# Keys and values through TensorE tiles of 64x32, eight key and value loads in flight, and vp evacuated in two halves: memory attention and SwiGLU on one core

## The chip, the cores and the metric

One core of a Trainium2 chip runs the whole kernel as one program. The metric is the device time of one execution in microseconds. The kernel before took 909.95 us, the median of three runs (909.52, 909.95 and 912.1). Below, "engine" is one of TensorE (PE), VectorE (DVE), ScalarE (ACT), GpSimd (POOL) and the queue of SyncE (SP), which here issues the DMAs.

## The reference, cut to what matters

```
# q, k, v: (8 batches, 8 heads, 576 rows, 64), phi: (8, 8, 576, 32)
a = exp(phi - max(phi, rows));  a = a / (sum(a, rows) + 1e-9)
k_m = einsum('bhsm,bhsd->bhmd', a, k)        # 32 x 64 for each batch and head
v_m = einsum('bhsm,bhsd->bhmd', a, v)
s = q @ k_m.T / sqrt(64);  s = exp(s - max(s));  attn = s / (sum(s) + 1e-9)
x = (attn @ v_m), heads side by side         # 4608 tokens x 512
xn = x / sqrt(mean(x*x) + 1e-6) * rms_g
out = (silu(xn @ w_gate) * (xn @ w_val)) @ w_out     # 512 -> 1536 -> 512
```

All inputs are float32; the weights come in as float64 words that the kernel takes apart itself.

## The kernel before, in words

The kernel never builds x. It keeps the attention weights of each token (32 for each of 8 heads, so 256 for two head groups) and multiplies the weights by v_m first: vp = v_m @ (w_gate | w_val). The gate and value of a token are then its attention weights times vp. Float32 products in this second part are made from a high and a low half (the names end in h and l), in three matmuls each.

**Stage 1** (the pool ps1, lines 434 to 786) works through the 8 batches, and batches 2i and 2i+1 form pair i. For each batch `prep` loads phi, takes its maximum over the rows (`mc`, `mt`, `mx`, `mr`: a reduction, a transpose, a reduction, a transpose back), subtracts it and writes exp to `e_bd`. There each head pair (of 4) has 9 chunks of 64 columns: rows 0 to 63 of the partitions are the first head, with its exponentials in columns 0 to 31 and zeros beside them, and rows 64 to 127 are the second head, with zeros first. `kv_steps` multiplies: each matmul takes such a 128x64 block as its stationary operand and 64 columns each of k and v of both heads as the moving one, so 36 matmuls a batch (line 573) accumulate into `kvp`. `sums` (588) adds up the exponentials with a column of ones, over partial sums `es` that POOL has made (554, 556). `post1` (596 to 605) divides and masks: `im` is the reciprocal by a mask of heads, `kb` and `vb` are k_m and v_m by it. `turn` transposes them, `post2` copies them to `km` and `vt`, `self_products` and `post3` make the gram matrix of v_m that the norm needs, and `vg`, v_m scaled by rms_g, goes into `vm` in high and low halves (pairs 0 and 1) or to DRAM (`vgd`, pairs 2 and 3).

For the pairs 0 and 1 stage 1 also makes the scores: `q_steps` transposes q, `score_steps` multiplies by `km` into the PSUM tile `S`, and takes max, exp and sum. `x_steps` then transposes the attention weights (`tp`, `at`), makes the sums of squares with the gram matrix (`xp`, `ssq`), takes the reciprocal root by Newton steps on DVE (`rinv`, `u`), spreads it with `rp`, and splits the result into `ath` and `atl`. Beside this, `convert` turns a loaded weight block (`raw`) from float64 words into a float32 pair: five or six DVE operations, the source lines 345 to 385 in each (`ex`, `mi`, `w`), two ACT operations between, a cast on ACT (402) and a subtraction on POOL (403).

**Stage 2** (the pool ps2) loops over i from 0 to 47: two halves of the feed-forward width for each of 12 blocks by two pairs, twice. `vw_steps(i)` makes `vp` (840: 12 matmuls into one PSUM tile of 2x2x256 floats a partition, with one buffer) and `evac` splits it, per half of the partitions, into `xh` (an ACT cast, 853) and `xl` (a DVE subtraction, 854). `gv_steps` multiplies by `ath` and `atl` into `pg` and `pv` (876), takes silu and the product, and splits `hf` into `hh` and `hl`. `out_steps` multiplies by the output weights into `po` (918) and adds into `acc` (925). The pairs 2 and 3 have their scores made here, between the steps.

**What sets the order.** Each step has a due time in the table `PRM` (K_AT: a batch's products; KD: how far ahead of them each key and value tile is loaded; S_AT: scores; X_AT: the x steps; CV: conversions). Steps are recorded in that order, and a scheduler then places the instructions of each engine in one fixed row, which the chip runs in order. The input loads of stage 1 (`load`) stand in a chain of their own on SP: none is issued ahead of the one recorded before it. A load of `kv` (two DMAs, k and v of a head pair) also waits until the matmuls that read the buffer's former tile are through; there are 5 such buffers. On the same queue stand the stores of `vgd`, of the gram matrix (`gd`) and of converted weights (`wd`, `od`), and a store that waits for its data holds up every load behind it.

Of the kernel before, what the change touches and what calls it, by code (L numbers as in the profile page):

```python
# [31 lines left out]
    KD=[-29.43, -117.84, -35.71, -6.98, -5.97, -14.4, 0.19, -2.47, -27.9, -16.32, -19.75, -7.2, -11.66, -11.87, -26.49, -25.1, -22.49, -18.77, -23.35, -24.43, -11.42, -13.48, -5.56, -9.46, -16.01, -22.32, -10.3, -18.0, -66.41, -9.39, -2.35, -17.36],  # L32
    QD=[5.05, 6, 3, 5, 23.44, 20.6, 19, 15.8],
# [18 lines left out]
    B=[2, 2, 2],  # L52
# [38 lines left out]
def kernel(  # L91
# [25 lines left out]
    nc = tc.nc  # L117
# [28 lines left out]
    km_late = {b: persist.tile([P, HP, 64], F32, name=f"km{b}") for b in range(2 * G, B)}  # L146
    ssqs = {}
# [280 lines left out]
    with ExitStack() as c1:  # L428
# [8 lines left out]
        hmask = sb.tile([P, 2], F32, name="hmask", bufs=1)  # L437
        for g in range(4):
            for c in range(2):
                nc.vector.memset(hmask[32 * g:32 * g + 32, c:c + 1], float(g % 2 == c))  # L440
# [50 lines left out]
        def prep(b, hp0=0, hp1=HP):  # L491
# [46 lines left out]
            def s3():  # L538
                ph = st["phi", b][:, hp0:hp1]
                e = e_bd[b % 2]  # L540
                for h in range(2):
                    nc.scalar.activation(
                        e[64 * h:64 * h + 64, hp0:hp1, :, 32 * h:32 * h + 32],
                        ph[64 * h:64 * h + 64], AF.Exp,
                    )

            def s4():
                e = e_bd[b % 2]
                n = PRM["ESN"][b]
                es = []  # L550
                if n:
                    t = sk.tile([P, HP, 2, 64], F32, tag="es", name=f"es{b}")
# [9 lines left out]
        def kv_steps(b):  # L562
            j = b % 2

            def chunk(cc, c0, c1):
                def f():
                    if (cc, c0) == (0, 0):
                        st["kvp", b] = ps.tile([P, 2, 256], F32, tag="kx", name=f"kvp{b}", bufs=PRM["B"][1])
                    kvp = st["kvp", b]
                    for c in range(c0, c1):  # L570
                        for par in range(2):
                            hp = 2 * cc + (par ^ j)
                            nc.tensor.matmul(  # L573
                                kvp[64 * par:64 * par + 64, cc, 0:128],
                                e_bd[j][:, hp, c, :],
                                st["kv", b, hp][:, :, 64 * c:64 * c + 64],
                                start=(c == 0), stop=(c == NT - 1),
                            )
                return f

            def sums():
                kvp = st["kvp", b]
                for cc in range(2):
                    for par in range(2):
                        hp = 2 * cc + (par ^ j)
                        es = st["es", b]
                        for i, x in enumerate(es):
                            nc.tensor.matmul(
                                kvp[64 * par:64 * par + 64, cc, 128:129],
                                x[:, hp, :], ones, start=(i == 0), stop=(i == len(es) - 1),  # L590
                            )

            def post1():
# [4 lines left out]
                im = sb.tile([P, 2, 2], F32, tag="im", name=f"im{b}")  # L598
                nc.vector.tensor_tensor(
                    out=im, in0=si.broadcast_to([P, 2, 2]),  # L600
                    in1=hmask.unsqueeze(1).broadcast_to([P, 2, 2]), op=ALU.mult,
                )
                st["kb", b] = [sb.tile([P, 2, 2, 64], F32, tag=f"{x}b", name=f"{x}b{b}") for x in "kv"]
                for i in range(2):
                    nc.vector.tensor_tensor(
                        out=st["kb", b][i],
                        in0=kvp[:, :, 64 * i:64 * i + 64].unsqueeze(2).broadcast_to([P, 2, 2, 64]),
                        in1=im.unsqueeze(3).broadcast_to([P, 2, 2, 64]),
                        op=ALU.mult,
                    )  # L610

            def turn():
                kb = st["kb", b]
                st["kvt", b] = tp = ps.tile([P, 2, HP, 64], F32, tag="kx", name=f"kvt{b}", bufs=PRM["B"][1])
                for i in range(2):
                    for cc in range(2):
                        nc.tensor.transpose(
                            out=tp[:, i, 2 * cc:2 * cc + 2, :].rearrange("p s m -> p (s m)"),
                            in_=kb[i][:, cc].rearrange("p h d -> p (h d)"), identity=ident,
                        )  # L620

            def post2():
                tp = st.pop(("kvt", b))
                km = km_late.get(b)
                if km is None:
                    km = sb.tile([P, HP, 64], F32, tag="km", name=f"km{b}", bufs=4)
                nc.scalar.copy(km, tp[:, 0])
# [478 lines left out]
```

## Time and profile before

| what | us |
|---|---|
| median of three runs | 909.95 |
| the profiled execution | 910.09 |
| its span, first to last instruction | 908.3 |
| PE busy | 838.9 |
| DVE busy | 592.2 |
| ACT busy | 421.1 |
| POOL busy | 286.6 |

The span of the profiled execution is 1.8 us shorter than the execution, which lies 0.14 us from the median. The mean granted clock of TensorE is 0.969. The share of busy time says little by itself here, since two stages with different limits follow one another: stage 2 begins with the first `pg` matmul at 156.9 us. A row of the windows view gives, for a stretch of time, the busy us of each engine with the number of its instructions in brackets, the granted clock, the busy share of the DMA engines and GB/s. In the view by shapes a row gives line, engine, operation, output and inputs, count, then busy us and the mean ns of one, then the idle time just before them and what ended it. The chain of waits is the work that ended last, followed back from the end; "issue" in it is time in which the engine waited for nothing that the profile shows. A float32 matmul that isn't a transpose appears in the trace as two pieces, so the 36 products of a batch are 72 MATMULs.

### The profile page before, as it was taken

The numbers are of one execution on the slowest core, as the hardware profiler recorded it, in microseconds if no ns is written. First come the engines' busy times: TensorE is split into PE (matmuls) and PEld (weight loads), VectorE is DVE, ScalarE is ACT, GpSimd is POOL, SyncE is SP. The second block draws the span as 40 slices with busy tenths as digits, with TensorE's granted clock in tenths as the row PEclk, the third lists the DMA queues.
The fourth block names the chain that finished last, engine by engine and source line by source line (L and its number), as shares of the span: only waits on it lengthen the run. The fifth ranks groups of instructions, "written<-read, shape, count | busy, mean of one in ns | idle before, by whom it ended". The sixth has DMA issues, their size and how long they took to land.

```text
span 908.3 us, 15828 instructions
## 1 busy us (share of the span) xinstructions
PE 838.9 (92%) x6207; PEld 744.3 (82%) x6207; DVE 592.2 (65%) x1026; ACT 421.1 (46%) x717; POOL 286.6 (32%) x242
## 2 busy tenths in 40 slices
PE   4989485899989999899999999999999999999997
PEld 3777474889887899788888997798889999999996
DVE  5577968997898877988754655632445455454543
ACT  2656433777766464665543343254424333243330
POOL 3463745333333324234242241412112121121120
PEclk9889887999999999999999999999999999999999
DMA  8976543553464341634214134411204012040046
GB/s 284 324 254 236 201 157 96 182 185 86 153 166 132 106 119 61 165 110 153 89 58 140 35 94 128 97 55 47 93 1 140 1 48 93 1 140 1 1 111 144
DMA packets 81506, 106.41 MB, mean 117 GB/s; under 512 B 34324, under 2 KB 52248, under 8 KB 81432
## 3 DMA queue, kind: packets, MB, share of 16 engines
q1 hardware_dynamic: 81432, 105.41, 37.6%
q8 instruction: 49, 0.80, 0.4%
q14 instruction: 25, 0.20, 0.1%
HBM read 73.93 MB, written 31.46 MB: 116 GB/s over the span
## 4 chain that ended last, share of the span: by engine, by line
PE 74%; DVE 14%; issue 4%; DMA 4%; ACT 3%; POOL 1%; SPq 0%; DVEq 0%; ACTq 0%; POOLq 0%
PE po L918 29%; PE pv L876 14%; PE pg L876 14%; PE vp L840 7%; PE kvp L573 3%; PE xp L235 1%; DVE mi L365 1%; DVE xl L854 1%; DVE ex L345 1%; DVE w L385 1%; ACT xh L853 1%; PE qtp L685 1%; DVE mi L369 1%; DVE acc L925 1%; DMA phi<-in_phi_dram 1%
## 5 line engine op out<-in xcount | busy, mean ns | idle before, releaser
L899 POOL TENSOR_TENSOR hl<-hf,hh 128x512 fp32r<-128x512 f32 (+1 forms) x96 | 139.6, 1454 | 410.9 <-ACT hh L898 399.6
L925 DVE TENSOR_TENSOR acc<-po,acc 128x512 f32<-128x512 f32 x180 | 123.1, 687 | 130.2 <-PE po L918 129.5
L918 PE MATMUL po<-oh,hh 128*128 128x512 f32 x432 | 173.6, 403 | 3.6 <-DVE acc L925 2.6
L918 PE MATMUL po<-oh,hl 128*128 128x512 f32 x432 | 171.1, 396 | 0.0
L918 PE MATMUL po<-ol,hh 128*128 128x512 f32 x432 | 170.9, 396 | 0.0
L884 ACT ACTIVATE sg<-pg 128x256 f32<-128x256 f32 x192 | 77.7, 409 | 163.2 <-PE pg L876 144.2
L854 DVE TENSOR_TENSOR xl<-vp,xh 64x1024 fp32r<-64x1024 f32 x96 | 117.2, 1220 | 45.9 <-ACT xh L853 44.4
L885 DVE TENSOR_TENSOR hf<-pv,sg 128x256 f32<-128x256 f32 x192 | 85.3, 453 | 73.0 <-PE pv L876 51.1
L853 ACT CAST xh<-vp 64x1024 fp32r<-64x1024 f32 x96 | 96.6, 1007 | 51.7 <-PE vp L840 21.6
L898 ACT CAST hh<-hf 128x512 fp32r<-128x512 f32 (+1 forms) x96 | 64.6, 673 | 82.3 <-DVE hf L885 57.0
L918 PEld LDWEIGHTS po<-oh,hl 128*128 128x128 f32 x432 | 81.5, 189 | 19.5
L918 PEld LDWEIGHTS po<-oh,hh 128*128 128x128 f32 x432 | 81.5, 189 | 19.3 <-DVE acc L925 4.5
L876 PE MATMUL pg<-ath,xh 128*128 128x320 f32 (+1 forms) x384 | 86.6, 299 | 7.9 <-ACT xh L853 6.3
L918 PEld LDWEIGHTS po<-ol,hh 128*128 128x128 f32 x432 | 81.7, 189 | 11.5 <-DMA ol<-od 0.2
L840 PE MATMUL vp<-wh,vm 128*128 128x256 f32 x384 | 85.5, 288 | 4.8 <-DVE at L212 2.3
L876 PE MATMUL pv<-ath,xh 128*128 128x320 f32 (+1 forms) x384 | 84.7, 300 | 4.7 <-DVE hf L885 4.6
L876 PE MATMUL pg<-ath,xl 128*128 128x320 f32 (+1 forms) x384 | 85.7, 296 | 0.0
L876 PE MATMUL pv<-atl,xh 128*128 128x320 f32 (+1 forms) x384 | 84.7, 296 | 0.0
L876 PE MATMUL pg<-atl,xh 128*128 128x320 f32 (+1 forms) x384 | 84.4, 297 | 0.0
L876 PE MATMUL pv<-ath,xl 128*128 128x320 f32 (+1 forms) x384 | 83.3, 296 | 0.0
L876 PEld LDWEIGHTS pg<-ath,xh 128*128 128x128 f32 x384 | 63.8, 190 | 13.3 <-ACT xh L853 6.6
L840 PEld LDWEIGHTS vp<-wh,vm 128*128 128x128 f32 x384 | 66.0, 191 | 8.4 <-DVE xl L854 3.0
(129 smaller groups left out, 1377.5 us busy)
## 6 DMA issues: line engine op xcount, KB each, us to landing
kv<-in_k_dram SPq DMA_DIRECT2D x32, 288.0 KB, 4.8
kv<-in_v_dram SPq DMA_DIRECT2D x32, 288.0 KB, 5.4
out_dram<-acc SPq DMA_DIRECT2D x72, 128.0 KB, 2.4
raw<-in_moe_w_gate_dram SPq DMA_DIRECT2D x12, 512.0 KB, 4.8
raw<-in_moe_w_val_dram SPq DMA_DIRECT2D x12, 512.0 KB, 3.7
wd<-wh SPq DMA_DIRECT2D x12, 512.0 KB, 3.0
wd<-wl SPq DMA_DIRECT2D x12, 512.0 KB, 4.1
raw<-in_moe_w_out_dram SPq DMA_DIRECT2D x12, 512.0 KB, 3.6
```

The costliest lines, as they stand in the source:

```text
L235: nc.tensor.matmul(xp[64 * j:64 * j + 64, P * cc:P * cc + P], st["at"][:, t, cc, 64 * j:64 * j + 64], gb[:, j, cc], start=True, stop=True,)
L573: nc.tensor.matmul(kvp[64 * par:64 * par + 64, cc, 0:128], e_bd[j][:, hp, c, :], st["kv", b, hp][:, :, 64 * c:64 * c + 64], start=(c == 0) ...
L840: nc.tensor.matmul(vp[:, cc, e, :], lhs(l), r[:, 2 * cc + e, :], start=(n == 0), stop=(n == 2),)
L853: nc.scalar.copy(xh[rows], src)
L854: nc.vector.tensor_tensor(out=xl[rows], in0=src, in1=xh[rows].bitcast(F32), op=ALU.subtract)
L876: nc.tensor.matmul(pt[:, :N], l[:, cc, b, half * P:half * P + P], r[:, b, cc, t0:t0 + n, :].rearrange("p t x -> p (t x)"), start=(m == 0), ...
L884: nc.scalar.activation(sg[:, :N], pg[:, :N], AF.Silu)
L885: nc.vector.tensor_tensor(out=hf[:, :, b, :], in0=pv[:, :N].rearrange("p (t x) -> p t x", x=64), in1=sg[:, :N].rearrange("p (t x) -> p t x ...
L898: nc.scalar.copy(hh, hv)
L899: nc.gpsimd.tensor_tensor(out=hl, in0=hv, in1=hh.bitcast(F32), op=ALU.subtract)
L918: nc.tensor.matmul(po, l[:, tt, :], r, start=(m == 0), stop=(m == 5))
L925: nc.vector.tensor_tensor(out=accs[key], in0=po, in1=accs[key], op=ALU.add)
```

## The change

The exponentials are stored without zeros (`e_all`, 32 columns a chunk, both heads' rows under one another), so one ACT operation of 128 partitions writes what two of 64 wrote, and `es` is half as wide. Each product is now that of one head: 64 rows of partitions, 32 columns of exponentials, 128 columns of k and v. A batch has 72 of them, in eight tiles (four head pairs by two heads), and `kvp` has 2x512 floats a partition, one half for each head, in a PSUM tag of its own with one buffer. For this room `S` has one buffer in place of two. The sums go from 1 column by 64 to 1 by 32, twice as many. `post1` has no mask: one multiplication makes the whole of `kb`. The zeros are now in `km` and `vt`, which POOL clears once at the start; two transposes in place of four, and four ACT copies of 64x128 in place of two of 128x256, fill their other parts. There are 8 buffers for key and value tiles, and none is loaded later than 12 units (KL) ahead of its batch, less half a unit for each further head pair. In stage 2 `vp` is two tiles of 2x256 floats with two buffers, and `evac` has four casts and four subtractions of 64x512 in place of two each of 64x1024.

```
+    KL=-12.0,
-    B=[2, 2, 2],
+    B=[2, 2, 1],
...
-        e_bd = [sk.tile([P, HP, NT, 64], F32, name=f"e_bd{i}", bufs=1) for i in range(2)]
-        nc.vector.memset(e_bd[0], 0.0)
-        nc.gpsimd.memset(e_bd[1], 0.0)
-        nc.gpsimd.memset(gb, 0.0)
+        e_all = [sk.tile([P, HP, NT, M], F32, name=f"e{i}", bufs=1) for i in range(2)]
+        kms = {b: sb.tile([P, HP, 64], F32, name=f"km{b}", bufs=1) for b in range(2 * G)}
+        vts = [sb.tile([P, HP, 64], F32, name=f"vt{i}", bufs=1) for i in range(2)]
+        for t in (kms[0], vts[0], kms[1], vts[1], kms[2], kms[3], gb):
+            nc.gpsimd.memset(t, 0.0)
...
-            t = sk.tile([P, 2, S], F32, tag="kv", name=f"kv{b}_{hp}", bufs=5)
+            t = sk.tile([P, 2, S], F32, tag="kv", name=f"kv{b}_{hp}", bufs=8)
...
-                for h in range(2):
-                    nc.scalar.activation(
-                        e[64 * h:64 * h + 64, hp0:hp1, :, 32 * h:32 * h + 32],
-                        ph[64 * h:64 * h + 64], AF.Exp,
-                    )
+                nc.scalar.activation(e_all[b % 2][:, hp0:hp1], ph, AF.Exp)
...
-                        for par in range(2):
-                            hp = 2 * cc + (par ^ j)
-                            nc.tensor.matmul(
-                                kvp[64 * par:64 * par + 64, cc, 0:128],
-                                e_bd[j][:, hp, c, :],
-                                st["kv", b, hp][:, :, 64 * c:64 * c + 64],
+                        for s in range(HP):
+                            for h in range(2):
+                                rows = slice(64 * h, 64 * h + 64)
+                                nc.tensor.matmul(
+                                    kvp[32 * s:32 * s + 32, h, 0:128],
+                                    e_all[j][rows, s ^ j, c, :],
+                                    st["kv", b, s ^ j][rows, :, 64 * c:64 * c + 64],
...
-                nc.vector.tensor_tensor(
-                    out=im, in0=si.broadcast_to([P, 2, 2]),
-                    in1=hmask.unsqueeze(1).broadcast_to([P, 2, 2]), op=ALU.mult,
-                )
-                for i in range(2):
-                    nc.vector.tensor_tensor(
-                        out=st["kb", b][i],
+                nc.vector.tensor_tensor(
+                    out=kb.rearrange("p i h d -> p h i d"),
+                    in0=kvp[:, :, :128].rearrange("p h (i d) -> p h i d", i=2),
+                    in1=si.unsqueeze(3).broadcast_to([P, 2, 2, 64]),
...
-                nc.scalar.copy(km, tp[:, 0])
-                nc.scalar.copy(vt, tp[:, 1])
+                for i, x in enumerate((km, vt)):
+                    for h in range(2):
+                        rows = slice(64 * h, 64 * h + 64)
+                        nc.scalar.copy(
+                            x[rows, :, 32 * h:32 * h + 32],
+                            tp[rows, P * i:P * i + P].rearrange("p (s m) -> p s m", m=M),
+                        )
...
-                    ev.append((K_AT[b] + PRM["KD"][b * HP + hp], lambda b=b, hp=hp: load_kv(b, hp)))
+                    ev.append((K_AT[b] + min(PRM["KD"][b * HP + hp], PRM["KL"] + 0.5 * hp), lambda b=b, hp=hp: load_kv(b, hp)))
...
-                if cc == 0:
-                    vw[i] = [ps.tile([P, 2, 2, 256], F32, tag="vw", name=f"vp{i}", bufs=1)]
+                vp = ps.tile([P, 2, 256], F32, tag="vw", name=f"vp{i}_{cc}", bufs=2)
...
+            for cc, vp in enumerate(vw[i]):
+                halves = ((slice(0, 64), vp[:64]), (slice(64, P), vp[64:, ::-1, :]))
+                for rows, src in halves:
+                    nc.scalar.copy(xh[rows, cc], src)
+                for rows, src in halves:
+                    nc.vector.tensor_tensor(
+                        out=xl[rows, cc], in0=src, in1=xh[rows, cc].bitcast(F32), op=ALU.subtract
+                    )
```

On PE, the products of batch 0 begin like this before; the names are those of the program with a running number, `kv_0` is the tile of head pair 0, and the sizes are those of the output:

```order
L523 MATMUL mr_2_168<-ident,mb_2_166 128x64
L573 MATMUL kvp_221<-kv_0_141,e_bd_131 64x128
L573 MATMUL kvp_221<-kv_1_144,e_bd_131 64x128
L573 MATMUL kvp_221<-kv_0_141,e_bd_131 64x128
L573 MATMUL kvp_221<-kv_1_144,e_bd_131 64x128
```

and like this now:

```order
L524 MATMUL mr_2_172<-ident,mb_2_170 128x64
L571 MATMUL kvp_229<-kv_0_146,e_126 32x128 x2
L571 MATMUL kvp_229<-kv_1_149,e_126 32x128 x2
L571 MATMUL kvp_229<-kv_2_176,e_126 32x128 x2
L571 MATMUL kvp_229<-kv_3_186,e_126 32x128 x2
L571 MATMUL kvp_229<-kv_0_146,e_126 32x128 x2
```

Two head pairs took turns, and the other two followed; now all four tiles of a batch are in use from its first product to its last, so their buffers come free together.

On SP, the loads for the last two batches and for the weight blocks of n = 1 stood so before (`raw` of w_val is the last load that the conversions of stage 1 wait for):

```order
L412 DMA wd_82<-wh_1363 128x1024
L412 DMA wd_82<-wl_1364 128x1024
L657 DMA vgd_75<-vg_1359 128x256
L659 DMA gd_66<-gram_1304 128x256
L298 DMA kv_3_1450<-in_k_dram 128x576
L298 DMA kv_3_1450<-in_v_dram 128x576
L298 DMA kv_1_1562<-in_k_dram 128x576
L298 DMA kv_1_1562<-in_v_dram 128x576
L298 DMA kv_2_1604<-in_k_dram 128x576
L298 DMA kv_2_1604<-in_v_dram 128x576
L298 DMA raw_1685<-in_moe_w_val_dram 128x4x256
```

and stand so now:

```order
L301 DMA raw_1662<-in_moe_w_gate_dram 128x4x256
L301 DMA kv_3_1731<-in_k_dram 128x576
L301 DMA kv_3_1731<-in_v_dram 128x576
L301 DMA kv_1_1844<-in_k_dram 128x576
L301 DMA kv_1_1844<-in_v_dram 128x576
L301 DMA kv_2_1852<-in_k_dram 128x576
L301 DMA kv_2_1852<-in_v_dram 128x576
L301 DMA raw_2028<-in_moe_w_val_dram 128x4x256
L648 DMA vgd_75<-vg_1619 128x256
L650 DMA gd_66<-gram_1569 128x256
```

The stores `vgd` of batch 5 and `gd` of pair 2, which stood ahead of these loads, now stand behind them.

On DVE, between the last Newton step for pair 1 (`rinv_71`) and the first subtraction of stage 2 (`xl`) there stood before, with `at` the scaling by rinv, `raw_1724` the output weights of block 0 and `w` the last operation of a conversion:

```order
L212 TENSOR_TENSOR at_1503<-at_1503,rp_0_1760 128x1024
L212 TENSOR_TENSOR at_1503<-at_1503,rp_4_1770 128x1024
L385 TENSOR_TENSOR w_1_1735<-mi_1_1731,ex_1_1726 128x512
L212 TENSOR_TENSOR at_1503<-at_1503,rp_8_1776 128x256
L345 TENSOR_SCALAR ex_0_1828<-raw_1724 128x512
L365 TENSOR_SCALAR mi_0_1833<-raw_1724 128x512
L347 TENSOR_SCALAR ex_0_1828<-ex_0_1828 128x512
L369 SCALAR_TENSOR_TENSOR mi_0_1833<-raw_1724,mi_0_1833 128x512
L358 SCALAR_TENSOR_TENSOR ex_0_1828<-raw_1724,ex_0_1828 128x512
L854 TENSOR_TENSOR xl_1823<-vp_1809,xh_1822 64x1024
```

and there stand now, where `w_0_2196` and `w_1_2353` (output weights of blocks 0 and 1) are already done inside the Newton steps, and `raw_2193` and `raw_2350` are w_gate and w_val of block 2:

```order
L215 TENSOR_TENSOR at_1818<-at_1818,rp_0_2111 128x1024
L361 SCALAR_TENSOR_TENSOR ex_2_2424<-raw_2193,ex_2_2424 128x512
L215 TENSOR_TENSOR at_1818<-at_1818,rp_4_2122 128x1024
L215 TENSOR_TENSOR at_1818<-at_1818,rp_8_2128 128x256
L388 TENSOR_TENSOR w_2_2435<-mi_2_2429,ex_2_2424 128x512
L348 TENSOR_SCALAR ex_2_2497<-raw_2350 128x512
L368 TENSOR_SCALAR mi_2_2517<-raw_2350 128x512
L350 TENSOR_SCALAR ex_2_2497<-ex_2_2497 128x512
L372 SCALAR_TENSOR_TENSOR mi_2_2517<-raw_2350,mi_2_2517 128x512
L843 TENSOR_TENSOR xl_2176<-vp_0_2161,xh_2175 64x512 x2
```

Three more weight blocks (output weights of block 1, w_gate of block 2, and most of w_val of block 2) are thus converted ahead of the first `xl`, and the Newton steps of pair 1 stand behind the `kb` of batch 7, where they stood ahead of it.

More of the change, by code (lines that the diff above doesn't have):

```diff
@@ L579, in chunk @@
                 return f
             def sums():
[L582 to L587, printed above, removed]
+                kvp, es = st["kvp", b], st["es", b]
+                for i, x in enumerate(es):
+                    for s in range(HP):
+                        for h in range(2):
+                            rows = slice(64 * h, 64 * h + 64)
@@ L588, in sums @@
                             nc.tensor.matmul(
-                                kvp[64 * par:64 * par + 64, cc, 128:129],
-                                x[:, hp, :], ones, start=(i == 0), stop=(i == len(es) - 1),
+                                kvp[32 * s:32 * s + 32, h, 128:129],
+                                x[rows, s ^ j, :], ones[rows], start=(i == 0), stop=(i == len(es) - 1),
                             )
@@ L612, in turn @@
+                    in1=si.unsqueeze(3).broadcast_to([P, 2, 2, 64]),
+                    op=ALU.mult,
+                )
             def turn():
                 kb = st["kb", b]
[L614 removed]
+                st["kvt", b] = tp = ps.tile([P, 512], F32, tag="kx", name=f"kvt{b}", bufs=PRM["B"][1])
                 for i in range(2):
[L616 to L620, printed above, removed]
+                    nc.tensor.transpose(
+                        out=tp[:, P * i:P * i + P], in_=kb[:, i].rearrange("p h d -> p (h d)"), identity=ident,
+                    )
```

57 lines of the change are left out of this document (22 added, 35 removed).

## The prediction

> **What bounds the kernel now.** I read the page first, then the busy time in stretches, then the chain of waits in time order, and last the waits of SP's queue. Stage 2, from about 157 us on, is TensorE's; stage 1 isn't any one engine's:
>
> ```profile
> span 908.3 us, 15828 instructions
> ```
> ```profile
> 0.00:20.00 20.00, 10.07 (x87) 8.37 (x88) 9.78 (x22) 4.01 (x5) 6.92 (x11) 0.91 0.87 295
> 20.00:40.00 20.00, 16.25 (x205) 13.82 (x202) 11.19 (x23) 11.55 (x21) 9.18 (x11) 0.83 0.94 317
> 40.00:60.00 20.00, 20.00 (x330) 17.12 (x332) 16.03 (x26) 15.15 (x25) 8.33 (x10) 0.91 0.81 258
> 60.00:80.00 20.00, 16.54 (x212) 14.18 (x208) 11.88 (x24) 9.02 (x15) 11.94 (x13) 0.83 0.88 308
> 80.00:100.00 20.00, 18.33 (x297) 15.09 (x297) 18.72 (x48) 13.94 (x26) 10.77 (x12) 1.00 0.33 105
> 100.00:120.00 20.00, 9.30 (x89) 7.89 (x88) 19.21 (x38) 6.07 (x14) 14.89 (x18) 0.66 0.56 198
> 120.00:140.00 20.00, 16.09 (x229) 14.11 (x227) 10.80 (x37) 7.02 (x12) 5.29 (x5) 0.91 0.57 185
> 140.00:160.00 20.00, 8.90 (x81) 8.00 (x78) 19.50 (x33) 8.47 (x17) 12.02 (x10) 0.73 0.40 108
> 160.00:180.00 20.00, 17.57 (x116) 16.32 (x115) 19.35 (x28) 15.03 (x26) 7.63 (x5) 0.93 0.55 190
> 180.00:200.00 20.00, 18.30 (x153) 16.61 (x152) 19.16 (x31) 13.44 (x27) 7.51 (x6) 1.00 0.64 188
> ...
> 240.00:300.00 60.00, 53.74 (x379) 46.31 (x378) 52.89 (x85) 39.08 (x67) 22.43 (x16) 1.00 0.52 157
> ...
> 700.00:800.00 100.00, 100.00 (x620) 91.16 (x620) 51.85 (x77) 35.52 (x58) 20.06 (x14) 1.00 0.14 49
> ```
>
> The third number of a row is PE's busy time, the fifth without its bracket VectorE's (after PE and weight loads), and the last three are the granted clock, the DMA share and GB/s. From 700 to 800 us PE is busy all the time. Up to 80 us the DMA engines are 0.81 to 0.94 busy, from 40 to 60 us PE is full, from 80 to 120 us and from 140 to 200 us VectorE is (18.7 to 19.5 of 20). From 120 to 140 us nobody is: VectorE has 10.8. So the time falls by as much as stage 1 gets shorter, less what stage 2 gives back. Where stage 1 waits for loads, the chain and SP's waits say:
>
> ```profile
> 59.19 5.37 DMA kv<-in_v_dram
> ...
> 118.89 2.18 PE kvp L573 x40
> ...
> 124.05 6.40 DMA raw<-in_moe_w_val_dram
> ```
> ```profile
> SPq L298 <- PE kvp L573: 33.7, 11, 10.6
> SPq L657 <- POOL vg L633: 30.0, 4, 13.2
> ```
>
> SP stood 33.7 us, 11 times, for the products to free a buffer, and 30.0 us, 4 times, in front of a store of `vgd` whose data POOL hadn't made. Two of the stops came out in the chain: the v tile that it waits 5.37 us for at 59 us, and the weight block that it waits 6.40 us for at 124 us.
>
> **The change part by part.**
>
> *Eight buffers.* The load at 59 us stood behind the fifth buffer; with eight, and with none loaded later than 12 units ahead, it no longer does. The DMA rows to 80 us add up to 70.0 us of work (17.4, 18.8, 16.2, 17.6), so at most 10.0 us can be pulled forward there. I take the wait, **-5.4 us**. Next late is PE, full from 40 to 60 us; so between 0 and -10. Phi, on the same queue, goes behind one to three tiles more in batches 1 and 2; that delays the early maxima by a few us at most and is covered as long as PE has products to do: 0.
>
> *The order on SP.* The block of w_val now stands ahead of the `vgd` store that held SP for 13.2 us. VectorE stood for it:
>
> ```profile
> 130.55 0.43 DVE L345 TENSOR_SCALAR ex<-raw 128x512 int32<-128x512 int32 x1 [3.98 <-DMA raw<-in_moe_w_val_dram]
> ```
>
> Of the 6.40 us VectorE had 3.98 idle, and it is VectorE that carries the chain there: **-4.0 us** (0 to -6.4).
>
> *The smaller operations.* These rows have the prices:
>
> ```profile
> L573 PE MATMUL kvp<-kv,e_bd 128*64 128x128 f32 x576 | 47.8, 320 | 4.4 <-DMA kv<-in_v_dram 2.9 <-DVE ssq L248 0.9 <-DMA rg_rows<-in_moe_rms_g_dram 0.5
> L556 POOL TENSOR_TENSOR es<-es,e_bd 128x512 f32<-128x512 f32 x14 | 17.8, 1270 | 0.8
> L542 ACT ACTIVATE e_bd<-phi 64x1152 f32<-64x1152 f32 x14 | 16.3, 1163 | 17.4 <-DVE rg L456 10.4 <-issue 5.1 <-DVE phi L532 1.8
> L599 DVE TENSOR_TENSOR im<-si,hmask 128x4 f32<-128x4 f32 x8 | 4.8, 597 | 0.2
> L605 DVE TENSOR_TENSOR vb<-kvp,im 128x256 f32<-128x256 f32 x8 | 3.3, 411 | 0.0
> ```
>
> VectorE loses `im` and one of two products in each batch, 0.60 + 0.41 = 1.0 us. Batches 4 to 7 fall where VectorE or its chain is the bound: 4 x 1.0 = **-4.0 us** (0 to -8, for all eight). ScalarE loses one of two operations of 1.16 us a batch and POOL half of es (1.27 us goes to between 0.64 and 1.27); neither is full anywhere in stage 1, so 0. ScalarE's four copies for two cost it at most two more small operations a batch, in idle time: 0.
>
> *The products on PE* are the open price. One tile works through a 128-column piece in about 0.11 us, and two tiles at a time halve that; this is seen by the single-tile transposes beside the products, and the sums show that a second tile's pieces start before the first tile's are all through:
>
> ```profile
> 118.72 2.35 PE L573 MATMUL kvp<-kv,e_bd 128*64 128x128 f32 x40
> 121.23 0.22 PE L588 MATMUL kvp<-ones,es 128*64 128x1 f32 x1
> 121.28 0.20 PE L588 MATMUL kvp<-ones,e_bd 128*64 128x1 f32 x1
> 121.31 0.20 PE L588 MATMUL kvp<-ones,es 128*64 128x1 f32 x1
> 121.34 0.20 PE L588 MATMUL kvp<-ones,e_bd 128*64 128x1 f32 x1
> 122.66 1.09 PE L184 MATMUL tp<-ident,a 128*128 128x128 f32 x8
> ```
>
> Eight transposes in 1.09 us, the last of some 0.28, make 0.116 us each; 40 pieces of products in the chain's 2.18 us make 54.5 ns each. `es` of the next group starts between the `e_bd` of the last, about 30 ns apart, so PE lets a few blocked pieces be overtaken. Before, 576 pieces x 54.5 ns = 31.4 us. Now there are 1152, twice as many of equal length: with two tiles at a time 62.8 us, with four 31.4, with all eight 15.7. I take 20 ns a piece, 23.0 us, since a few overtaken pieces are enough to keep more than four tiles going once they are out of step. A batch is then 144 x 20 = 2.88 us in place of 3.92; for the batches 2, 3 and 6, which the chain runs through on PE, that is 3 x 1.04 = **-3.1 us**. From both sides: all eight at once saves 2.0 us a batch (-6), two at a time costs 3.9 a batch. The Trainium skill speaks against a gain here: "TensorE: Matmul & The Clock Gate", Part 1, the section on the 56 ns gap, says that start-to-start never falls below about 25 ns however small a matmul is; by it the estimate is 1152 x 25 = 28.8 us, so that at most 0.3 us a batch is won, and the sum is 2 us smaller. The rows above show no sustained spacing under some 30 ns, so the trace neither bears this out nor contradicts it.
>
> *One buffer for S and kvp.* The scores of the next head pair now wait until VectorE has read the last. The scheduler put other products between in all but a few places; one pass of VectorE there is some 1.5 us, and I take it as hidden (0 to +4).
>
> *The weight blocks ahead of stage 2.* Three more conversions stand ahead of the first `xl` than before, and the Newton steps moved behind `kb` of batch 7. The rows of one conversion:
>
> ```profile
> 143.30 0.42 DVE L605 TENSOR_TENSOR kb<-kvp,im 128x256 f32<-128x256 f32 x1
> ...
> 148.17 1.17 DVE L345 TENSOR_SCALAR ex<-raw 128x512 int32<-128x512 int32 x1
> ...
> 154.62 1.21 DVE L854 TENSOR_TENSOR xl<-vp,xh 64x1024 fp32r<-64x1024 f32 x1
> ...
> 156.46 0.43 DVE L345 TENSOR_SCALAR ex<-raw 128x512 int32<-128x512 int32 x1
> ...
> 157.25 1.23 DVE L854 TENSOR_TENSOR xl<-vp,xh 64x1024 fp32r<-64x1024 f32 x1
> ...
> 160.65 0.69 DVE L385 TENSOR_TENSOR w<-mi,ex 128x512 f32<-128x512 f32 x1
> ```
>
> One takes 161.34 - 156.46 - 1.23 = 3.65 us there, and 6.45 us without its last step at 148 us. So `xl`, before 11.3 us behind `kb`, comes some 3 x 3.65 = 11 us later behind it than before. These conversions are missing later, where VectorE is as full (160 to 200 us) or nearly (240 to 300 us) and PE stood idle: 2.4 + 1.7 us from 160 to 200, 6.3 from 240 to 300. I take 7 of these 10.4 us as returned: **+4 us** (0 to +11).
>
> *Evacuation by halves.* Prices by nearest rows:
>
> ```profile
> L925 DVE TENSOR_TENSOR acc<-po,acc 128x512 f32<-128x512 f32 x180 | 123.1, 687 | 130.2 <-PE po L918 129.5
> L854 DVE TENSOR_TENSOR xl<-vp,xh 64x1024 fp32r<-64x1024 f32 x96 | 117.2, 1220 | 45.9 <-ACT xh L853 44.4
> L853 ACT CAST xh<-vp 64x1024 fp32r<-64x1024 f32 x96 | 96.6, 1007 | 51.7 <-PE vp L840 21.6 <-DVE xl L854 20.6 <-PE pv L876 8.6
> L402 ACT CAST wh<-w 128x512 fp32r<-128x512 f32 x24 | 14.8, 619 | 18.1 <-DVE w L385 5.9 <-PE kvp L573 5.2 <-PE vp L840 4.5
> ```
>
> VectorE pays 4 x 0.687 - 2 x 1.220 = 0.31 us more for each of 48 i, 14.8 us in all, ScalarE 4 x 0.619 - 2 x 1.007 = 0.46. PE covers all of it from about 300 us on; until then some 8 i lie where VectorE is full, 2.5 us, and the halves let the next `vp` and `pg` begin sooner, worth at most a us or two. I take **+1 us** (-2 to +3; +14.8 if no cover held).
>
> The sum against the profiled execution: -5.4 - 4.0 - 4.0 - 3.1 + 4 + 1 = -11.5, so 910.09 - 11.5 = 898.6 us. That execution lies 0.14 us over the median, 909.95, and 898.5 is the forecast beside it.
>
> **The rivals.**
>
> *More comes out of stage 1.* With eight tiles at once (-6 for -3.1) and the whole 10 us of DMA room (for 5.4), and with conversions that fit into VectorE's idle time (120 to 140 us has 9.2 of it) so that `xl` is not late (0 for +4), the sum is -11.5 - 2.9 - 4.6 - 4 = -23: 887 us. For it speaks that stage 1 has 43 us of idle VectorE up to 160 us; against, that the chain changes engine every few us, so that something else is late at once.
>
> *The gain is given back before stage 2.* `xl` waits for the blocks of w_gate and w_val ahead of it in VectorE's row. If their loads come late, 11 us late with nothing returned (+11 for +4) and two us for S, the sum is -11.5 + 7 + 2 = -2.5, 907.5 us: no difference to be told. For it: these loads stand behind stores that wait for POOL, as the 30.0 us show.
>
> *Slower: two tiles at a time.* If a product's two pieces follow one another and hold up what is behind them, each batch costs 7.85 us on PE, 3.9 more. On the chain are the batches 2, 3, 4 and 6: 15.7 for the -3.1 that I took, so -11.5 + 3.1 + 15.7 = +7.3: 917 us. It decides from 27 ns a piece on, where the products cost as much as before. For it: the trace never shows more than two at a time. Against: the overtaking above.
>
> *Slower: evacuation.* With VectorE's 14.8 us uncovered, +13.8 more than taken: 912 us. PE's full row at 700 us with VectorE at 51.85 of 100 speaks against it.
>
> That the change doesn't do what it says is out: the order of the instructions shows 32-column products, 8 tiles and 64x512 evacuations.
>
> **How the numbers follow.** My forecast, 898.5 with a few us either way, has 0.55; more out of stage 1 0.18; given back 0.12; two tiles 0.11; evacuation 0.04. The measurement tells 0.3%, 2.7 us, from no change. Faster by more: 0.55 + 0.18 less a little of the forecast's edge, 0.73. The same: most of "given back", 0.10. Slower: 0.11 + 0.04 and the worse half of what is given back, 0.17. The range leaves out the ends: from 884 (the large gain and 3 us) to 912.
>
> **What would show it.** In the changed profile: the first `pg` of stage 2 near 147 us, from 156.9; SP's wait for `kvp` far under 33.7 us; no wait of VectorE for w_val; pieces of `kvp` at 14 to 27 ns, a batch under 3.9 us; PE's idle time from there to 300 us under 10 us; `xl` near 0.69 us by four. The prediction is wrong if a batch of products takes over 4 us of a warm PE, if the first `pg` isn't before 154 us, or if PE has new gaps after 300 us.

## The result, and the profile after

The changed kernel takes 939.6 us (median) against 909.7 for the kernel before: ratio 1.0326, interval 1.0289 to 1.0362. The forecast was 898.5, from 884 to 912, and 0.73 for faster. It went the other way, and past every rival. One execution of e4 (1040.5 us) and one of e13 (1047.5 us) ran at a mean granted clock of 0.75 and are left out below; with it e4's median is the 917.9 us of the expectations.

First the span, and then the busy time in four stretches, of the kernel before and of the changed one. The cuts are the first `pg` of each, 300, 600 and the end; the columns are those of the rows above.

```profile
span 936.6 us, 17590 instructions
```
```profile
0.00:156.90 156.90, 112.40 (x1485) 95.50 (x1485) 114.16 (x239) 73.84 (x131) 78.05 (x86) 0.86 0.66 221
156.90:300.00 143.10, 132.54 (x931) 118.37 (x932) 127.04 (x199) 98.96 (x168) 53.21 (x37) 0.98 0.51 154
300.00:600.00 300.00, 290.80 (x1965) 256.92 (x1965) 208.36 (x381) 141.77 (x243) 95.21 (x78) 0.99 0.35 103
600.00:908.30 308.30, 303.20 (x1830) 273.49 (x1828) 142.65 (x209) 106.55 (x177) 60.12 (x42) 1.00 0.20 60
```
```profile
0.00:172.50 172.50, 107.18 (x2273) 78.06 (x2274) 104.44 (x225) 70.50 (x143) 66.87 (x95) 0.81 0.66 222
172.50:300.00 127.50, 118.03 (x830) 106.63 (x829) 105.82 (x179) 89.33 (x164) 43.62 (x33) 0.98 0.38 118
300.00:600.00 300.00, 283.18 (x1913) 248.37 (x1912) 224.21 (x415) 147.59 (x275) 90.11 (x73) 0.98 0.33 104
600.00:936.60 336.60, 329.51 (x1981) 297.26 (x1979) 165.19 (x281) 125.12 (x238) 71.86 (x52) 0.99 0.23 66
```

Of the 28.3 us by which the span grew, 15.6 are a later first `pg` (172.5 for 156.9). After it PE is busy 730.7 us (118.03 + 283.18 + 329.51) for 726.5, 4.2 more for the same products, and idle 33.4 (764.1 - 730.7) for 24.9, 8.5 more. So stage 1 lost more than half, and stage 2 the rest. The first `xl` is later still, by 20.4 us (174.98 for 154.62): the first `pg` now needs only half of `vp`, and after four such products PE stands 2.8 us for `xl`. In stage 1 no engine has more to do: PE 107 us, VectorE 104, both less than before.

The waits of SP and VectorE up to 180 us in the changed kernel, and behind them VectorE's around `phi` before (total, times, longest):

```profile
SPq L301 <- PE kvp L571: 21.2, 3, 13.4
```
```profile
DVE mc L500 <- DMA phi<-in_phi_dram: 33.1, 7, 7.8
...
DVE ex L348 <- DMA raw<-in_moe_w_gate_dram: 6.2, 3, 3.5
```
```profile
DVE phi L532 <- PE mr L523: 16.2, 6, 5.8
...
DVE mc L499 <- DMA phi<-in_phi_dram: 4.4, 2, 4.0
```

SP waits less for the products, as forecast. VectorE waits 33.1 us for `phi`, 4.4 before. Not all of it is new idle time: before, it waited 16.2 us for PE's transposes (`mr`) in front of the subtraction, now 1.1, so the two waits together grew by 13.6. The loads are hardly late: those of the batches 1 to 6 are issued 0.7 us sooner to 2.3 later, that of batch 6 at 68.96 us, at 69.67 before. What changed is where VectorE stands in its row when it asks for them. The same place in time order, before and after: `mc` is the pass for the maxima of batch 6, `phi` the subtraction for batch 5.

```profile
70.12 1.35 DVE L532 TENSOR_TENSOR phi<-phi,mr 128x1152 f32<-128x1152 f32 x1 [4.74 <-PE mr L523]
...
77.22 2.19 DVE L499 TENSOR_REDUCE mc<-phi 128x128 f32<-128x1152 f32 x1
```
```profile
75.58 2.08 DVE L500 TENSOR_REDUCE mc<-phi 128x128 f32<-128x1152 f32 x1 [6.94 <-DMA phi<-in_phi_dram]
...
81.19 1.29 DVE L533 TENSOR_TENSOR phi<-phi,mr 128x1152 f32<-128x1152 f32 x1
```

Before, batch 5 is subtracted first and its exponentials follow; the next batch's maxima come 7 us later, when their load has landed (5.8 us after its issue at 69.67). Now the scheduler has the maxima of the next batch ahead, for each of the batches 1 to 6. VectorE goes in order, so the subtraction of batch 5, whose data lie there, waits behind a load for batch 6. The chain of the changed kernel shows it for the maxima of the batches 5 and 6, and then a second thing:

```profile
48.34 4.11 DMA phi<-in_phi_dram
52.48 2.20 DVE mc L500
...
61.36 1.22 DVE phi L533
...
68.96 6.60 DMA phi<-in_phi_dram
75.58 2.08 DVE mc L500
...
81.27 1.22 DVE phi L533
...
150.41 0.42 DVE kb L596
...
157.79 6.23 DMA raw<-in_moe_w_gate_dram
164.04 0.43 DVE ex L348
...
165.81 1.16 DVE at L215
...
175.06 0.60 DVE xl L843
```
```profile
PE rp L207 <- DVE rinv L279: 11.6, 1, 11.6
```

`kb` of batch 7 comes at 150.4 us, 143.3 before. From there to the first `xl` (174.98) it takes 24.6 us, 11.3 before. Between them stand the Newton steps of pair 1, some 0.17 us each, but with steps of weight conversions between them and one behind a load of w_gate: PE waits 11.6 us for the last. Before, they were through at 143.2, just ahead of `kb`.

### The profile page after: what moved, and what is told of

The parts are those of the page before. It is cut to its first block, busy times and chain, and to the rows that moved or that the text cites. A ratio compares the mean times of both kernels' runs of the same rounds, so it can differ in the third digit from the quotient of the medians.

```text
span 936.6 us, 17590 instructions
## 1 busy us (share of the span) xinstructions
PE 837.9 (89%) x6991; PEld 730.3 (78%) x6991; DVE 599.7 (64%) x1097; ACT 432.6 (46%) x820; POOL 272.5 (29%) x251
## 4 chain that ended last, share of the span: by engine, by line
PE 66%; DVE 17%; DMA 6%; issue 6%; ACT 4%; POOL 1%; SPq 0%; DVEq 0%; ACTq 0%; POOLq 0%
PE po L909 28%; PE pv L867 13%; PE pg L867 13%; PE vp L829 5%; DMA phi<-in_phi_dram 3%; DVE xl L843 2%; DMA raw<-in_moe_w_gate_dram 2%; DVE w L388 2%; DVE mi L372 2%; DVE ex L348 2%; PE xp L238 2%; DVE mi L368 1%; DVE acc L916 1%; DMA q<-in_q_dram 1%; PE kvp L571 1%
## 5 line engine op out<-in xcount | busy, mean ns | idle before, releaser
L843 DVE TENSOR_TENSOR xl<-vp,xh 64x512 fp32r<-64x512 f32 x192 | 132.0, 687 | 33.6 <-ACT xh L841 24.8
L841 ACT CAST xh<-vp 64x512 fp32r<-64x512 f32 x192 | 111.5, 581 | 18.4 <-PE pv L867 10.6
L829 PE MATMUL vp<-wh,vm 128*128 128x256 f32 x384 | 88.8, 288 | 11.1 <-DVE xl L843 9.4
L909 PEld LDWEIGHTS po<-ol,hh 128*128 128x128 f32 x432 | 81.9, 189 | 11.6
L829 PEld LDWEIGHTS vp<-wh,vm 128*128 128x128 f32 x384 | 67.1, 191 | 15.1 <-issue 6.2
L867 PEld LDWEIGHTS pv<-ath,xh 128*128 128x128 f32 x384 | 63.9, 192 | 11.9 <-DVE hf L876 5.8
```

Source lines behind the costliest of these rows:

```text
L829: nc.tensor.matmul(vp[:, e, :], lhs(l), r[:, 2 * cc + e, :], start=(n == 0), stop=(n == 2),)
L841: nc.scalar.copy(xh[rows, cc], src)
L843: nc.vector.tensor_tensor(out=xl[rows, cc], in0=src, in1=xh[rows, cc].bitcast(F32), op=ALU.subtract)
L867: nc.tensor.matmul(pt[:, :N], l[:, cc, b, half * P:half * P + P], r[:, b, cc, t0:t0 + n, :].rearrange("p t x -> p (t x)"), start=(m == 0), ...
L909: nc.tensor.matmul(po, l[:, tt, :], r, start=(m == 0), stop=(m == 5))
```

## The experiments

The kernel before ran beside each; its medians there are 909.3 to 909.6. The ratios below are to it.

| run | median, us | ratio, interval |
|---|---|---|
| the change | 939.6 | 1.0326 (1.0289 to 1.0362) |
| e1 five buffers | 943.0 | 1.0374 (1.0345 to 1.0403) |
| e2 maxima behind the subtraction | 924.2 | 1.0160 (1.0134 to 1.0185) |
| e3 whole evacuation | 938.7 | 1.0317 (1.0286 to 1.0348) |
| e4 before, evacuation by banks | 917.2 | 1.0089 (1.0063 to 1.0115) |
| e5 Newton ahead of conversions | 932.3 | 1.0239 (1.0214 to 1.0265) |
| e6 both edges | 917.6 | 1.0081 (1.0058 to 1.0104) |
| e7 both, whole evacuation | 914.4 | 1.0051 (1.0033 to 1.0068) |
| e9 before, four operations | 915.6 | 1.0064 (1.0045 to 1.0083) |
| e10 first xl ahead too | 915.5 | 1.0064 (1.0041 to 1.0086) |
| e11 e10 with halves | 918.2 | 1.0089 (1.0061 to 1.0117) |
| e12 e10 with late loads | 924.0 | 1.0160 (1.0132 to 1.0187) |
| e13 e7, tile by tile | 915.4 | 1.0064 (1.0042 to 1.0085) |
| e14 e10, w_out on POOL | 907.3 | 0.9977 (0.9960 to 0.9994) |
| e15 before, w_out on POOL | 910.8 | 1.0010 (0.9992 to 1.0028) |

**Why stage 1 was late (e1, e2).** My theory is the order on VectorE; the rival, the queue. e1 changes only `bufs=8` to `bufs=5`; e2 adds an order edge, and records the five steps of a batch's maxima no sooner than the former batch's:

```
+                with tc.issue_after(st["sub", b - 1]) if ("sub", b - 1) in st else nullcontext():
+                    nc.vector.tensor_reduce(
...
+                st["sub", b] = sub.ins
...
+                    ev[-5:] = [(max(t, prev + 0.01 * i + 0.01), f) for i, (t, f) in enumerate(ev[-5:])]
```

> The changed kernel with five key/value buffers in place of eight, all else as changed. Theory A (order): with eight buffers the order of VectorE has the maxima of the next batch (mc) ahead of the subtraction of the batch before (phi); VectorE then stands for a load of phi, 33.1 us in 7 waits against 4.4 in 2, and the exponentials come 2 to 19 us late. With five buffers the row has the old order for the batches 1 and 3 to 7, so the waits for phi fall under 12 us, the first pg comes near 155 to 160 us (177.3 in the changed kernel) and the time is 905 to 920. Theory B (the queue): the early loads (KL) put phi behind more tiles, whatever the number of buffers; then the waits stay over 25 us and the time over 930. Theory C (evacuation): the halves cost the 8 us of PE idle between 300 and 500 us that are new; those would stay here.

> The changed kernel, eight buffers, with the maxima of batch b on VectorE held in the order behind the subtraction of batch b-1 (an order edge, and the five steps of a batch recorded no sooner than it). Theory A (order): exponentials are no longer behind the next phi load; first pg near 155 to 162 us, time 908 to 922. Theory B (the queue): phi itself comes late, so VectorE waits as long, only a step later; first pg stays near 175, time 930 to 942.

e2 took 15.4 us off. The waits of VectorE for `phi` and the two marks in its profile:

```profile
DVE mc L501 <- DMA phi<-in_phi_dram: 10.6, 3, 5.9
```
```profile
137.41 0.42 DVE L598 TENSOR_TENSOR kb<-kvp,si 128x256 f32<-128x256 f32 x1
```
```profile
162.05 1.38 DVE L848 TENSOR_TENSOR xl<-vp,xh 64x512 fp32r<-64x512 f32 x2
```

`kb` of batch 7 is 13.0 us earlier than in the change and 5.9 earlier than before: part of the gain that I had summed for stage 1 is there, once this order is back. The queue as the main cause falls: `phi` of batch 6 is issued at 69.36 us in e2, no sooner, and the subtraction for batch 5 comes at 72.41 in place of 81.19. My expectation of e1 fell too: with five buffers the old order was back but for batch 2, and VectorE waited 17.9 us for `phi`, but the time wasn't back. The early due times need the eight buffers; with five SP stands for the products, and with it every load behind:

```profile
SPq L301 <- PE kvp L571: 65.8, 8, 14.0
```

**Newton and conversions (e5, e6).** One edge holds the conversions recorded after the last multiplication of `at` behind it:

```
+                if (pr, t0) == (1, 8):
+                    gate.append(last.ins)
...
+                with tc.issue_after(gate[0]) if gate else nullcontext():
+                    f()
```

> The changed kernel with one order edge: of the weight conversions recorded after the last multiplication of at of pair 1, none stands ahead of it on VectorE; two blocks are then converted between kb of batch 7 and the first xl, as before, in place of seven. Theory D (second order loss): the twelve Newton steps of pair 1, interleaved with conversions, and the blocks behind them put the first xl 24.6 us behind kb of batch 7 in place of 11.3; with the edge it is 11 to 14 us behind, and the time 926 to 931 (939.6 less 9 to 13). Rival: those blocks come out of VectorE's later idle time in any order, so what xl gains the weights lose: 936 to 941.

> The changed kernel with both edges: maxima of batch b behind the subtraction of batch b-1 (924.2 us by itself), and the weight conversions behind the last at of pair 1. Theory A and D together: kb of batch 7 near 137 us, first xl near 149 to 151, time 911 to 915. If D is given back later: 921 to 926. If both losses were the same one seen twice: no better than 924.

These expectations, and that of e10, count each block twice: it is one block before, nearly four in the change, one and two thirds in e7. The edge by itself is worth 7.3 us, and 6.6 on top of the first; both times (932.3 and 917.6) lie between the ranges expected, and `xl` is 16.9 us behind `kb` (137.00 and 153.85 in e6), since the last `x` products, and with them the Newton steps, still end behind `kb`. The two losses are different ones, and their sum is 22 us of 29.9.

**The evacuation (e3, e4, e7, e8, e9).** e3 and e7 put back the former `evac` and its one tile; e4 and e8 (the same kernel, one run of 917.9 us, for its profile) put the new one into the kernel before; e9 keeps its tile and only splits the operations:

```
+            for cc in range(2):
+                halves = ((slice(0, 64), vp[:64, cc]), (slice(64, P), vp[64:, cc, ::-1, :]))
```

> The changed kernel with the former evacuation of vp: one tile of 2x2x256 with one buffer, two casts and two subtractions of 64x1024. Stage 1 is unchanged in code. Theory C (evacuation): 7 to 9 us less, 930 to 933, and PE's idle time from 300 to 500 us back from 14.7 to some 6 us. Rival: the halves cost nothing or win, and the idle time comes from conversions that stage 1 left over: 936 to 943.

> The kernel before with only the evacuation of vp by single banks: two tiles of 2x256 with two buffers, four casts and four subtractions of 64x512. Theory C (evacuation costs): 915 to 918, PE idle between 300 and 500 us up by 5 to 8 us. Rival (hidden, as I forecast at +1): 908 to 912. A third: the halves let the next vp begin sooner and win 2 to 4 us.

> As the run with both edges, and with the former evacuation of vp in whole tiles of two banks. Theory C (the halves cost some 8 us, as on the kernel before: 917.9 against 909.6): 903 to 907, faster than the kernel before. Rival (the halves cost nothing here, as in the changed kernel without edges: 938.7 against 939.6): 911 to 916.

> The kernel before with the evacuation by single banks once more, for a profile (918 us by time). Theory C: the added 8 us lie between the first xl and 600 us, as idle time of PE in front of vp or of po, while VectorE's row has four subtractions of 0.69 us for two of 1.22. Rival: they lie in stage 1, by another order.

> The kernel before with vp left as one tile of two banks and one buffer, but evacuated by four casts and four subtractions of 64x512, bank by bank. Theory C1 (the cost of the halves is VectorE's work: 2.74 us a vp in place of 2.44, 14.8 us in all, where VectorE is full): about as slow as with single banks, 915 to 919. Theory C2 (the cost is the tiles: two one-bank tiles with two buffers let vp go into PE's row early, where PE then waits for xl): no slower than before by more than 2 us, 907 to 912.

On the kernel before, the halves cost some 8 us (0.9%). On the changed one they cost 0.9 (e3, not to be told from nothing), with both edges 3.2 (e7). e3 isn't a clean measure: its first `xl` comes at 180.3 us, 5.3 later than in the change, and the time behind it is 4.7 us shorter. e9 has some 6 of the 8 with the old tile, so most of it is the price of twice the operations (C1), not of the tiles; the intervals overlap, and the other 2 us stay open. From 300 to 600 us, e8 first and then e9:

```profile
300.00:600.00 300.00, 284.87 (x1913) 250.41 (x1912) 218.75 (x412) 143.46 (x271) 94.19 (x77) 0.99 0.33 101
```
```profile
300.00:600.00 300.00, 286.85 (x1930) 252.08 (x1930) 218.10 (x419) 146.09 (x274) 95.08 (x78) 0.99 0.36 105
```

PE is idle 15.1 and 13.2 us there, 9.2 before. VectorE is busy 10 us more (the split is 14.8 us of work over the whole kernel), and PE did not cover it, though VectorE is idle a quarter of that time: what counts is when `vp` is free and `xl` there, not the share.

**What an earlier stage 2 is worth (e10, e11, e12).** e10 adds `if i == 0: gate.append(low.ins)` behind the first two `xl` to e7 and holds the conversions behind the latest gate; e11 has the halves in addition; e12 is e10 with `KL=-2.0`.

> The run with both edges and the whole evacuation (914.4 us), and the weight conversions recorded after the first xl held behind it on VectorE: none between kb of batch 7 and the first xl, in place of three. Theory D (what stands ahead of the first xl counts): first xl near 148 us in place of 154.3, time 907 to 911. Rival (the conversions are needed for po and PE waits for them a few us later): 912 to 916.

> The same with the evacuation by halves, as the change has it (with both edges alone 917.6 us). Theory D: 909 to 914. Rival: 916 to 919.

> The run with all edges and the whole evacuation, with KL at -2 in place of -12: key and value tiles are due as before, eight buffers kept. Theory B (early loads put phi behind more tiles and cost): kb of batch 7 some us sooner than 136.4, time 2 to 6 us under the run with KL at -12. Rival (early loads are what feeds the products; my sum had them at -5.4): kb later by 3 to 6 us and the time by as much. Neither: within 1.5 us.

e12 says that the early loads are worth 8.5 us with eight buffers (`kb` of batch 7 at 150.4 for 134.9). e10 has the first `xl` at 148.6, 5.7 us sooner than e7, and wins nothing; e11, at 918.2, is no better than e6. The stretches of e10:

```profile
0.00:151.20 151.20, 106.36 (x2273) 79.01 (x2273) 93.01 (x207) 66.62 (x136) 65.36 (x95) 0.83 0.69 236
151.20:300.00 148.80, 131.23 (x915) 117.50 (x915) 129.41 (x201) 98.92 (x166) 50.27 (x36) 0.96 0.47 143
300.00:600.00 300.00, 292.46 (x1958) 258.48 (x1959) 210.66 (x385) 141.79 (x242) 96.92 (x78) 0.99 0.35 103
600.00:914.40 314.40, 307.54 (x1848) 277.56 (x1846) 143.09 (x210) 108.04 (x180) 60.07 (x42) 0.99 0.20 59
```

Against the kernel before, the first `pg` is 5.7 us sooner, but PE is busy 731.2 us after it (4.7 more, at a lower granted clock), and idle 32.0 (7.1 more, most of it up to 300). VectorE did 93 us of work ahead of the first `pg`, 114 before. Most of that is work that the kernel no longer has (576 us in all for 592); 5 us more (483 for 478) were still to come when stage 2 began.

**The products, and VectorE's work (e13, e14, e15).** e13 turns the loops so that the chunks of one tile follow one another; e14 and e15 take one multiplication of each w_out block off VectorE:

```
-                    for c in range(c0, c1):
-                        for s in range(HP):
-                            for h in range(2):
+                    for s in range(HP):
+                        for h in range(2):
+                            for c in range(c0, c1):
```
```
-            on_pool = n < 2 and kind < 2 and PRM["CE"][n] & (1 << kind)
+            on_pool = kind == 2 or n < 2 and PRM["CE"][n] & (1 << kind)
```

> The run with both edges and the whole evacuation (914.4 us), with the products recorded tile by tile inside a step (for a head pair and a head, then its two or three chunks) in place of chunk by chunk over all eight tiles. So it tells what eight tiles at a time are worth. If the overlap needs neighbours in different tiles: pieces of a warm run go from 13.5 to 14.2 ns to 25 to 55 ns, a batch from 2 us to 4 to 8, and the time rises by 5 to 20 us. If a piece may overtake several blocked ones: spacing 14 to 20 ns, time within 2 us of 914.4.

> The run with the first xl ahead (915.5 us), with the last multiplication of each w_out block (0.69 to 1.1 us on VectorE, 12 blocks) on POOL. Theory E (VectorE's work up to 450 us is what stage 2 waits for, so a gain in stage 1 that isn't a gain of VectorE's work is given back): 5 to 9 us less, 906 to 911, with less PE idle time from 200 to 600 us (19.6 us). Rival (what is given back lies in the order of particular waits): 913 to 917.

> The same edit on the kernel before, as a control. Theory E: VectorE's row is full there too from 140 to 200 us and nearly from 350 to 450, so 3 to 7 us less, 902 to 906. Rival: 907 to 911.

A warm run of products on PE in the changed kernel, and one in e13:

```profile
64.56 1.37 PE L571 MATMUL kvp<-kv,e 64*32 64x128 f32 x80
```
```profile
62.22 1.72 PE L582 MATMUL kvp<-kv,e 64*32 64x128 f32 x84
```

The last piece takes some 0.27 us, so 80 pieces start (1.37 - 0.27) / 79 = 14 ns apart, all eight tiles at a time; e13 has 17 to 18 here, up to 30 in other stretches. e13's time is 1.0 us over e7's, within what the runs can tell, and `kb` of batch 7 stands at 136.3 for 136.4. So the fast products are true, and slowing them to about the 27 ns at which they would cost as much as before changes next to nothing.

e14 takes 8.2 us off e10, as theory E has it, and is the fastest of all, 0.2% under the kernel before. But the control, e15, wins nothing on the kernel before, where VectorE lost as much work. So E isn't shown: e14 has its last `kb` 4.5 us later than e10, and three quarters of what it won, by the two profiles, is PE's busy time for the same products: 725.0 us after the first `pg` (132.21 + 291.68 + 301.12) for 731.2, at a higher clock.

```profile
155.70:300.00 144.30, 132.21 (x926) 117.09 (x926) 125.40 (x197) 98.57 (x167) 58.98 (x43) 0.98 0.46 143
300.00:600.00 300.00, 291.68 (x1976) 259.22 (x1977) 207.82 (x378) 142.62 (x245) 103.02 (x84) 0.99 0.35 105
600.00:906.40 306.40, 301.12 (x1818) 271.80 (x1816) 142.66 (x209) 106.21 (x176) 60.08 (x42) 1.00 0.20 61
```

## Why the prediction was wrong, step by step

- **"Phi ... goes behind one to three tiles more ...; that delays the early maxima by a few us at most and is covered as long as PE has products to do: 0."** This is the step that failed. I priced the queue (the loads of the batches 1 to 6 are issued 0.7 us sooner to 2.3 later) and not the row of the engine that waits for it. The maxima of the next batch had moved ahead of the subtraction of this one, so the late `phi` held up exponentials and, through them, the products. 15.4 us (e2). Two of the three signs of being wrong came true: the first `pg` at 172.5 us, not before 154, and 23.9 us of idle PE behind 300 us, 14.3 before.
- **Weight blocks ahead of stage 2, +4.** I had seen that the Newton steps moved behind `kb`, and priced only the blocks, with 7 of 11 us returned. The steps came to stand between conversions, one of them behind a load; `xl` is 13.3 us later behind `kb` than before, and e5 and e6 give 7.3 and 6.6 back.
- **Evacuation by halves, +1 (-2 to +3).** Some 8 on the kernel before, 3.2 in e7: I took 8 of 48 i as uncovered, from VectorE's share, where PE's idle time to 600 us grew with it.
- **Eight buffers, -5.4.** SP's wait fell to 21.2, and e12 gives 8.5 us to the early due times. But with the former due times and eight buffers e12 has `kb` at 150.4, later than the 143.3 before, and no run has five buffers with the order back, so what the buffers themselves gained stays open.
- **The order on SP, -4.0.** Not gained: VectorE stands 6.2 us for w_gate now, where it stood 4.0 for w_val. It wasn't tried by itself.
- **VectorE's smaller operations, -4.0.** Not tried alone: VectorE's busy time ahead of the first `pg` fell from 114.2 to 104.4, fewer conversions included.
- **Products, -3.1, and the rival "two tiles at a time".** The rival was wrong, the pieces are faster than my 20 ns, and of the -3.1 little is left: e13, at 17 to 30 ns, is no slower than the runs can tell. The rule of "TensorE: Matmul & The Clock Gate" (the Trainium skill), Part 1, the section on the 56 ns gap, that start-to-start never drops below about 25 ns, doesn't hold for eight tiles of 64x32: 14 ns.
- **S with one buffer, 0.** Nothing speaks against it: up to 180 us the waits around it make 0.9 us on VectorE and 0.3 on PE. It wasn't tried by itself.

Together e2's edge, e6's and the whole evacuation give 25.2 of the 29.9 us back (939.6, 924.2, 917.6, 914.4). The gain of stage 1 was real but smaller than forecast: the terms ahead of `kb` make 16.5 us (5.4 + 4.0 + 4.0 + 3.1), and `kb` is 6.9 us sooner in e7. Which of these terms fell short, beside that of the order on SP, is not known. And still e7 is slower than before. Its account shows some of why: `xl` is 17.9 us behind `kb` there, and PE idles 5 us more after its first `pg`. From 150 to 300 us PE waits more for `sg`, the silu on ScalarE, in e7 (first) than before:

```profile
PE pg L880 <- ACT sg L888: 5.0, 4, 2.3
```
```profile
PE pg L876 <- ACT sg L884: 1.5, 1, 1.5
```

What holds up ScalarE there was not settled.

## What to carry to other kernels

Where a scheduler sets the order, price an edit by what now stands ahead of each step on the engine that will wait, above all operations on a load that comes later than the step behind them; here such a reordering cost 15.4 us, more than the 11.5 that the whole change was to gain. A gain ahead of a tuned stage is only worth what the stage can take up, so ask what work it will find undone. That an engine has idle time on the whole doesn't cover more operations on it.

## What the runs showed of the hardware

A short pause of PE can cost nearly twice its length. Three stretches of 4 us in e10, with PE's busy time first and the granted clock third from the end:

```profile
240.00:244.00 4.00, 2.15 (x12) 1.62 (x11) 2.81 (x4) 3.95 (x7) 1.98 (x2) 1.00 0.48 131
244.00:248.00 4.00, 4.00 (x14) 3.41 (x14) 3.88 (x6) 3.74 (x7) 1.97 (x3) 0.57 0.37 145
248.00:252.00 4.00, 4.00 (x24) 3.53 (x23) 3.37 (x7) 2.04 (x5) 1.29 (x1) 1.00 0.55 183
```

Of the first 4 us PE was idle 1.85; in the next 4 it is always busy, at a mean granted clock of 0.57, and gets through 14 matmuls, in the last through 24. So 1.85 us of idle time cost some 4 x (1 - 0.57) = 1.7 more. A whole idle window of about 3.4 us isn't needed for it, as "TensorE: Matmul & The Clock Gate" (the Trainium skill), Part 1, the section "What's actually happening", would have it.

Nor does every such pause cost it. At 573 us PE waits 2.3 us for `rinv` of a later pair in the kernel before and in e14, shown in this order:

```profile
572.00:576.00 4.00, 1.74 (x14) 1.54 (x13) 3.17 (x12) 0.00 (x0) 0.94 (x1) 0.97 0.61 140
576.00:580.00 4.00, 4.00 (x14) 3.20 (x13) 1.91 (x2) 1.14 (x2) 1.56 (x2) 0.60 0.00 1
```
```profile
572.00:576.00 4.00, 1.74 (x14) 1.45 (x13) 2.95 (x13) 0.00 (x0) 0.44 (x1) 1.00 0.57 131
576.00:580.00 4.00, 4.00 (x25) 3.29 (x23) 2.72 (x4) 1.14 (x2) 2.33 (x2) 1.00 0.25 59
```

The same 2.3 us cost a stretch at a low clock in the one and nothing in the other. In the profiles of the kernel before, the change, e7, e10 and e14 there are 14 pauses of 1.8 to 2.4 us behind the first `pg`, and nine of them were followed by a stretch at half clock; what decides it is not shown. By the rows above, PE's busy time behind the first `pg` times what is missing from the clock is some 5.6 us before, 11.2 in e10 and 5.6 in e14. That is most of why the same products took 726.5, 731.2 and 725.0 us, so part of what e14 won over e10 in these profiles may be luck with the clock.
